# A two-layer spectral and MLP kernel: other PSUM banks for the zero multiplies between the layers

## The chip, the cores and the metric

The kernel runs on one core of one Trainium2 chip. The metric is the device time of one execution in microseconds, as the median of several runs. A profile is one further execution, recorded instruction by instruction. The engines are named as in the profile: PE is TensorE (its matrix multiplies), PEld are the weight loads of the same engine, DVE is VectorE, ACT is ScalarE, POOL is GpSimd, SP is SyncE, which issues most of the DMAs.

## The reference

The input is a state x of 2048 rows by 512 columns in bf16. Two kinds of layer follow each other, twice:

```
x = x + _A_ref(_layernorm(x), A_w_r, A_w_i)           # rfft2, times a complex weight, irfft2
x = x + _B_ref(_layernorm(x), B_w1, B_w2, B_w3, B_w4) # gelu MLP with row shifts, then an MLP of width 1792
x = x + _A_ref(_layernorm(x), A_w_r, A_w_i)
x = x + _B_ref(_layernorm(x), B_w1, B_w2, B_w3, B_w4)
```

`_A_ref` is a two-dimensional Fourier transform over the 2048 rows and 512 columns, an elementwise product, and the transform back. `_B_ref` is a layernorm, a 512 by 512 product with gelu, shifts of the rows by one or two in each quarter of the columns, a second 512 by 512 product, a residual, a layernorm, and an MLP of width 1792.

## The kernel before

The 2048 rows lie in SBUF as 128 partitions times 16 "rows" q, so that `x_state` is a tile of 128 x 16 x 512. The Fourier transform over the rows is split in two: a product over the 128 partitions (`over_p`, lines 361 and 363, or `over_p_plain`, line 373), and later one over the 16 values of q. The layernorm ahead of the transform is folded in: the statistics of row q give a factor, and `scale_T` multiplies the Fourier table T by it into a tile `Tq` (line 348, on DVE). The multiply with `Tq` as the moving operand then does norm and transform at once.

The function `layer` runs twice. Each call works through a long list of operations written out by hand, ORDER_A for the first call and ORDER_B for the second. The list sets the order of the instructions on every engine: an engine takes its own instructions in that order, and only semaphore waits hold it up. An entry is a letter for the function, a number for the piece of work, often V or A for DVE or ACT, and after a point the PSUM bank in which the result lies. PSUM is one tile `ps` of 8 banks of 512 fp32 columns. An operation that fills two banks takes the named one and the next.

The end of ORDER_A belongs already to the Fourier transform of the second call. Its entries there are:

- `Q14`: `scale_T` for the piece 14, which is row 0 of the state. One DVE instruction on line 348.
- `O4.0`, `O6.3`, `O14.6`, `O15.7`: the products over the partitions, called fronts here. O4 (line 373) fills banks 0 and 1 with the rows 10 and 11, O6 (lines 361 and 363) banks 3 and 4, O14 bank 6, O15 bank 7.
- `G4A` and `G4V`: taking O4 out of PSUM. G4A is an ACT copy (line 151) of columns 256 to 511 of both banks into a tile `right`. G4V is `fold_V`: four DVE instructions (line 385) that add `right` to, and subtract it from, columns 0 to 255 of both banks, and write the tile `V`. It is called the fold here.
- `G6A`, `G14A`, `G15A` and `G15V`: copies of O6, of O14 and of one half each of O15 into `V`, on ACT (line 151) and DVE (line 149).
- `X4` and `X8`: zero multiplies (line 243). The function `fill` issues 4 or 8 multiplies of a tile of zeros by itself into columns 0 to 255 of the named bank. Nothing reads what they write.

The first entry of ORDER_B is `d15.3`: `over_d`, line 476, the product over the columns for the last block. Its weights are slices of `V` over all rows, so that it needs all of the copies and folds above. The rest of the second call hangs on it.

In this list `X4.0` stands behind G4A and ahead of G4V. The four zero multiplies write columns 0 to 255 of bank 0 before the fold reads them, so that the fold takes zeros for the left half of row 10. The tile framework sees the fold as a reader of what the zero multiplies wrote, and makes it wait for them. `X4.6` stands behind G14A, which reads the same bank 6, and is made to wait for that copy. `X8.2` writes bank 2, which nobody has read for a while.

Of the kernel before, what the change touches and what calls it, by code (L numbers as in the profile page):

```python
# [765 lines left out]
o12V U6 g20 W8.4 j6 W10.7 w21.1 g21 Q2 A5 B5 A10 L8 A8 W9.6 B10 L2 Q3 L15 A9 w25.4 g25 w23.6 w24.1 j5 L3 g23 B8 O1.3  # L766
L0 W11.7 j8 w27.5 j7 S1 G1A G1V A11 w22.3 g27 Q6 j10 Q0 B11 B9 j9 Q7 g24 j11 S2 Q9 g22 w26.0 O3.4 G3A Q4 Q5 Q10 O2.6
G3V G2A g26 W12.3 Q8 A12 G2V B12 j12 W15.5 A15 B15 j15 O0.3 G0A G0V S15 W13.7 A13 B13 j13 W14.2 Q11 O5.5 G5A S12 Q12
S13 Q15 O15.7 A14 B14 j14 S14 Q13 O4.0 G4A G15V O6.3 G6A X4.0 Q14 O14.6 G14A X4.6 G4V G15A X8.2
"""  # L770
ORDER_B = """
d15.3 d1.6 t15A d4.0 t1V q1.2 x1A d8.4 t4V t8A q15.6 x15A p1 q4.2 d12.0 t12A x4V p15 p4 d10.6 t10A b1.3 q12.1 x12V m1A
# [45 lines left out]
```

## Time and profile before

| What | us |
|---|---|
| median of 5 runs (354.36 to 354.87) | 354.82 |
| time of the profiled execution | 354.83 |
| its span, first to last instruction | 352.9 |
| PE busy in the span | 341.0 |
| ACT busy | 200.6 |
| DVE busy | 185.1 |
| PE idle just ahead of the zero multiplies at 188.18 | 0.69 |

The span is what lies between the first and the last instruction; 1.9 us of the execution lie around it. Times inside the profile count from the start of the span. A busy time is the union of an engine's instructions. Multiplies overlap in the pipeline, so the time between the starts of two neighbours says what one costs in a stream, and the duration of one (273 ns for one of 256 columns) is longer than that. A start follows from a wait: what an instruction waited for stands behind an arrow in a list of idle times.

### The profile page before, as it was taken

What the parts mean: (1) busy time and instruction counts of PE and PEld (TensorE: products, weight loads), DVE (VectorE), ACT (ScalarE), POOL (GpSimd) and SP (SyncE); (2) the same over time, 40 slices, a digit from 0 to 9 for tenths busy, and PEclk for the clock granted to TensorE, in tenths of its full rate; (3) what the DMA queues carried; (4) which work ended last, traced back from release to release, by engine and by line L of the source; (5) the groups of instructions that cost most, each with busy time, mean ns of one, the idle gap of its engine ahead of it and who ended that gap; (6) DMA issues with size and microseconds to landing.
All of it is one profiled execution on the core that took longest, in us unless ns stands there. A gap on an engine that the chain in (4) does not pass through costs nothing.

```text
span 352.9 us, 5586 instructions
## 1 busy us (share of the span) xinstructions
PE 341.0 (97%) x2124; PEld 188.8 (53%) x2124; DVE 185.1 (52%) x442; ACT 200.6 (57%) x355; POOL 68.2 (19%) x171
## 2 busy tenths in 40 slices
PE   8789899999999999999999999899999999999996
PEld 6667786444444444444557888544444444444442
DVE  4869989769270445176586988845732004001003
ACT  4989989585736406213416979976583660442400
POOL 1430037462030101001120004646050010000000
PEclk9999999999999999999999999999999999999999
DMA  7996936611030030300000000762004005101003
GB/s 226 265 304 229 365 123 120 119 31 31 1 61 0 0 61 12 77 0 2 1 2 0 2 2 2 121 105 59 17 2 90 0 0 106 45 0 46 0 30 104
DMA packets 47210, 24.35 MB, mean 69 GB/s; under 512 B 36816, under 2 KB 43984, under 8 KB 47184
## 3 DMA queue, kind: packets, MB, share of 16 engines
q1 hardware_dynamic: 46464, 21.84, 24.9%
q0 software_dynamic: 576, 2.11, 1.5%
q8 instruction: 16, 0.26, 0.3%
q14 instruction: 10, 0.08, 0.1%
q10 hardware_dynamic: 144, 0.07, 0.1%
HBM read 11.41 MB, written 2.10 MB: 38 GB/s over the span
## 4 chain that ended last, share of the span: by engine, by line
PE 79%; ACT 6%; DMA 5%; DVE 3%; issue 3%; SPq 1%; POOL 1%; POOLq 0%; DVEq 0%; ACTq 0%
PE ps L655 27%; PE ps L642 27%; PE ps L591 8%; PE ps L607 8%; ACT hT L151 2%; PE ps L476 2%; PE ps L540 2%; DVE x_state L560 2%; DMA W<-W 2%; ACT xn L270 1%; DMA x_state<-in_A_x_dram 1%; PE ps L500 1%; DMA xT<-xn 1%; PE ps L524 1%; PE ps L552 1%
## 5 line engine op out<-in xcount | busy, mean ns | idle before, releaser
L649 ACT ACTIVATE gT<-ps 128x1024 bf16<-128x1024 f32 x56 | 56.6, 1023 | 84.1 <-PE ps L642 81.0
L642 PE MATMUL ps<-xT,w 128*128 128x512 bf16 x448 | 99.3, 379 | 0.0
L655 PE MATMUL ps<-w,gT 128*128 128x512 bf16 x448 | 99.0, 379 | 0.0
L660 DVE TENSOR_TENSOR x_state<-ps,x_state 128x512 bf16<-128x512 f32 x32 | 21.5, 689 | 111.7 <-PE ps L655 111.7
L642 PEld LDWEIGHTS <-w 128*128 128x128 bf16 x448 | 43.8, 98 | 52.9
L655 PEld LDWEIGHTS <-gT 128*128 128x128 bf16 x448 | 43.7, 98 | 52.1
L615 DVE SCALAR_TENSOR_TENSOR xn<-xn,ln_c,ps 128x512 bf16<-128x512 bf16 x32 | 23.2, 745 | 18.1 <-PE ps L607 15.7
L270 ACT ACTIVATE junk<-xn 128x512 bf16<-128x512 bf16 x32 | 19.9, 624 | 16.8 <-DVE xn L615 16.8
L607 PE MATMUL ps<-w,hT 128*128 128x512 bf16 x128 | 29.1, 379 | 0.0
L591 PE MATMUL ps<-xT,w 128*128 128x512 bf16 x128 | 28.4, 379 | 0.4 <-DMA xT<-xn 0.4
L276 POOL TENSOR_SCALAR ln_mv<-ln_s 128x4 f32<-128x4 f32 x16 | 5.5, 344 | 90.7 <-DVE x_state L560 52.0
L560 DVE SCALAR_TENSOR_TENSOR x_state<-ps,x_state 128x512 bf16<-128x512 f32 x32 | 20.4, 685 | 2.6 <-PE ps L552 1.9
L257 DVE BATCH_NORM_STATS2 ln_st<-x_state 128x6 f32<-128x512 bf16 x28 | 18.7, 686 | 4.6 <-DMA x_state<-in_A_x_dram 4.4
L515 DVE TENSOR_TENSOR PB<-X,W 128x1024 bf16<-128x1024 bf16 (+1 forms) x40 | 21.0, 584 | 0.1
L591 PEld LDWEIGHTS <-w 128*128 128x128 bf16 x128 | 12.4, 98 | 15.7 <-issue 0.7
L607 PEld LDWEIGHTS <-hT 128*128 128x128 bf16 x128 | 12.5, 98 | 15.1
L270 ACT ACTIVATE xn<-x_state 128x512 bf16<-128x512 bf16 x32 | 19.7, 620 | 0.5 <-DVE x_state L560 0.2
L598 ACT ACTIVATE hT<-ps 128x512 bf16<-128x512 f32 x32 | 17.0, 601 | 1.4 <-PE ps L591 1.3
L540 PE MATMUL ps<-G,hT 128*128 128x256 bf16 x128 | 15.1, 273 | 2.1 <-DVE hT L149 1.2
L476 PE MATMUL ps<-FA,V 128*128 128x256 bf16 x128 | 16.1, 273 | 0.8 <-DMA W<-in_A_w_i_dram 0.8
L552 PE MATMUL ps<-Y,Tinv 128*128 128x256 bf16 x128 | 15.8, 272 | 0.7 <-DVE Y L149 0.5
L524 PE MATMUL ps<-TR,PB 128*128 128x128 bf16 x256 | 16.0, 219 | 0.0
(78 smaller groups left out, 389.5 us busy)
## 6 DMA issues: line engine op xcount, KB each, us to landing
w<-in_B_w_dram SPq DMA_DIRECT2D x2, 1792.0 KB, 12.0
W<-W POOLq DMA_DIRECT2D x4, 514.0 KB, 5.4
x_state<-in_A_x_dram SPq DMA_DIRECT2D x8, 256.0 KB, 6.5
out_dram<-x_state SPq DMA_DIRECT2D x16, 128.0 KB, 1.9
TR<-tab_TR SPq DMA_DIRECT2D x2, 512.0 KB, 5.7
w<-in_B_w_dram SPq DMA_DIRECT2D x2, 512.0 KB, 4.5
W<-in_A_w_r_dram SPq DMA_DIRECT2D x7, 128.5 KB, 5.7
W<-in_A_w_i_dram SPq DMA_DIRECT2D x7, 128.5 KB, 5.2
```

The lines of the kernel that those rows point to most:

```text
L270: K.nc.scalar.activation(out, src, ACT.Square, bias=0.0, scale=D ** -0.5, accum_out=self.s[:, i, 1:2])
L476: nc.tensor.matmul(oi[:, 1 - h], rhs=K.FA[:, t, h], lhsT=V[:, 2 * t + h, 2 * b:2 * b + 2].rearrange("d b q c -> d (b q c)"), start=(t == 0 ...
L515: nc.vector.tensor_tensor(t[:, :, 0:n], x, w, op=ALU.mult)
L540: nc.tensor.matmul(o[:, i, e * 256:(e + 1) * 256], lhsT=M[:, F, e, 2 * m + i, :], rhs=K.G[:, F, e, :], start=(F == 0 and e == 0), stop=(F ...
L560: nc.vector.scalar_tensor_tensor(K.x[:, q, :], ps.pop(("P", q)), 1.0, K.x[:, q, :], op0=ALU.mult, op1=ALU.add, accum_out=ln[g].s[:, i, 0:1])
L591: nc.tensor.matmul(o[:, i], lhsT=K.w1[:, t, j * P:(j + 1) * P], rhs=xT[g][:, :, t, :], start=(t == 0), stop=(t == 3))
L607: nc.tensor.matmul(o, lhsT=K.hT[:, j, st:st + P], rhs=K.w2[:, j, :], start=(j == 0), stop=(j == 3))
L615: nc.vector.scalar_tensor_tensor(xn[:, q, :], xn[:, q, :], ln[q // 4].c[:, q % 4:q % 4 + 1], ps.pop(("u", n)), op0=ALU.mult, op1=ALU.add, ...
L642: nc.tensor.matmul(o[:, i], lhsT=K.w3[:, c, t * P:(t + 1) * P], rhs=xT3[g][:, :, c, :], start=(c == 0), stop=(c == 3))
L649: nc.scalar.activation(gT[g][:, 2 * j:2 * j + 2, :], ps.pop(("w", k)), ACT.Gelu_apprx_tanh, bias=0.0, scale=1.0)
L655: nc.tensor.matmul(o, lhsT=gT[g][:, t, i * P:(i + 1) * P], rhs=K.w4[:, t, :], start=(t == 0), stop=(t == 13))
L660: nc.vector.tensor_tensor(K.x[:, q, :], ps.pop(("W", n)), K.x[:, q, :], op=ALU.add)
```

## The change

Three entries of ORDER_A name another bank. `fill` writes columns 0 to 255 of that bank, as before, and no other function is touched. The numbers and the order of the instructions on every engine stay the same.

```
-S13 Q15 O15.7 A14 B14 j14 S14 Q13 O4.0 G4A G15V O6.3 G6A X4.0 Q14 O14.6 G14A X4.6 G4V G15A X8.2
+S13 Q15 O15.7 A14 B14 j14 S14 Q13 O4.0 G4A G15V O6.3 G6A X4.2 Q14 O14.6 G14A X4.2 G4V G15A X8.0
```

The waits that the framework sets follow the banks:

- The first of the four multiplies of the first X4 no longer waits for ACT (G4A).
- The fold G4V no longer waits for PE. It still waits for ACT (`right`).
- O14's first weight load now waits for DVE (its `Tq`) and its first multiply for ACT. Before, the multiply waited for DVE alone.
- The second X4 no longer waits for ACT (G14A).
- X8's first weight load now waits for DVE (the fold, the last reader of bank 0), and its first multiply for ACT (G4A).
- The weight loads of d15 no longer wait for DVE. The first still waits for ACT.

```
 L243 Ldweights zeros
+L243 Matmult ps<-zeros 128x256
+...
+L243 Ldweights zeros [waits DVE_49]
 L243 Matmult ps<-zeros 128x256 [waits Activation_49]
...
-L476 Ldweights V [waits DVE_49,Activation_49]
+L476 Ldweights V [waits Activation_49]
...
-L385 TensorTensor V<-ps,right 128x2x32x4 [waits PE_49,Activation_49]
+L385 TensorTensor V<-ps,right 128x2x32x4 [waits Activation_49]
```

## The prediction

> **What bounds the kernel now.** I read the page first for the bound, then the chain of waits around the place of the change, then the timeline there, and last PE's waits behind it, to see whether a gain would reach the end. The page says that PE decides:
>
> ```profile
> PE 341.0 (97%) x2124; PEld 188.8 (53%) x2124; DVE 185.1 (52%) x442; ACT 200.6 (57%) x355; POOL 68.2 (19%) x171
> ```
>
> PE is busy in 341.0 of 352.9 us, so what shortens PE's queue or its few gaps shortens the kernel, and 11.9 us are all its gaps together. The change touches one stretch of some 3 us. The chain that ended last, asked for between 183 and 190 us, shows who decides there:
>
> ```profile
> 186.55 0.02 issue
> 186.57 1.57 ACT V L151 x2
> 188.14 0.04 issue
> 188.18 1.47 PE ps L243 x12
> 189.65 0.44 PE ps L476 x4
> ```
>
> PE's fronts end, ACT makes the two copies G6A and G14A until 188.14, 0.04 us later twelve zero multiplies start (the second X4 and X8), and behind them d15 starts the second layer. So the zero multiplies stand on the path: the first of them waits for a copy because it writes that copy's bank. The timeline of the same stretch gives the durations (start, length, engine, line; in brackets the idle time before and who ended it):
>
> ```profile
> 186.42 0.60 PE L243 MATMUL ps<-zeros 128*128 128x256 bf16 x4
> 186.56 0.29 DVE L348 TENSOR_SCALAR Tq<-T,ln_r 128x256 bf16<-128x256 bf16 x1 [0.48 <-POOL ln_r L294]
> ...
> 186.90 0.27 PE L361 MATMUL ps<-Tq,x_state 128*128 128x256 bf16 x1
> ...
> 187.13 1.42 DVE L385 TENSOR_TENSOR V<-ps,right 128x256 bf16<-128x256 f32 x4 [0.28 <-PE ps L243]
> 187.23 0.27 PE L363 MATMUL ps<-Tq,x_state 128*128 128x256 bf16 x1
> ...
> 188.18 1.47 PE L243 MATMUL ps<-zeros 128*128 128x256 bf16 x12 [0.69 <-ACT V L151]
> ...
> 189.49 0.38 PE L476 MATMUL ps<-FA,V 128*128 128x256 bf16 x2
> ```
>
> Three things are to be seen. PE runs twelve zero multiplies from 188.18 to the start of d15 at 189.49, that is 1.31 / 12 = 0.109 us each. The fold (line 385) sat 0.28 us until the first four zero multiplies had ended at 187.02, and ran from 187.13 to 188.55. And d15's inputs, the fold and ACT's last copy (ACT's stretch of three copies ran from 186.57 for 1.84 us, to 188.41), were ready almost a microsecond before d15 began.
>
> **The change, part by part.** The sum is made against the profiled execution: a span of 352.9 and a time of 354.83, which lies 0.01 above the median of the runs.
>
> First X4, bank 2 for bank 0. Without its wait it starts 0.11 after the last multiply of O6 (186.26), at 186.37 for 186.42. That is worth nothing: O14 behind it waits for `Tq` from Q14, which ends at 186.56 + 0.29 = 186.85, and O14 began at 186.90 by that. Bank 2 was filled by W14 and read by DVE at 183.94 for 0.69 us, long before.
>
> O14's wait for DVE moves from its first multiply to its first weight load. In the trace of before two streams begin with a weight load that really waited, and they bound it:
>
> ```profile
> 21.97 0.22 PEld L476 LDWEIGHTS <-V 128*128 128x128 bf16 x3 [1.08 <-ACT V L151]
> 21.98 0.39 PE L476 MATMUL ps<-FA,V 128*128 128x256 bf16 x2 [0.80 <-DMA W<-in_A_w_i_dram]
> ```
>
> ```profile
> 209.33 0.66 PEld L540 LDWEIGHTS <-hT 128*128 128x128 bf16 x7 [0.99 <-ACT hT L151]
> 209.34 0.83 PE L540 MATMUL ps<-G,hT 128*128 128x256 bf16 x6 [0.82 <-ACT hT L151]
> ```
>
> In both the multiply starts 0.01 us after its weight load. The other end is a load inside a stream, 189.38 to 189.49 for d15's first, 0.11 us. I take 0.01, the rows of a load that waited; the other only keeps the pace of the stream. O14 keeps its start, and its copy G14A stays behind G6A on ACT: no gain, no loss (at the far end 0.1 us on ACT, covered since d15 begins 0.7 us after ACT's last copy).
>
> [...]
>
> The fold. Its wait for PE goes; `right` was ready at 185.78 + 0.59 = 186.37. What is late next is its own engine: Q14 from 186.56 to 186.85. In the stretch at 182.47 three such scalings took 0.65 us together, (0.65 - 0.29) / 2 = 0.18 from one to the next, so the fold starts between 186.56 + 0.18 = 186.74 and 186.85, where 187.13 was. With 1.42 us it ends at 188.16 to 188.27. It could lose only if DVE had other work first, and the order of its instructions is unchanged.
>
> Second X4. Without its wait the four multiplies follow O14's last (187.23) at 187.34 and are issued by 187.78, inside what was PE's gap of 0.69 us. They leave the path: 4 x 0.109 = 0.44 us less behind the wait.
>
> X8, bank 0 for bank 2. It now waits for the fold instead of standing behind a wait for G14A. Queued behind its first weight load on PE is d15, and behind d15 all of the second layer. Release takes 0.05 (0.04 in the chain above; 186.85 to 186.90 at O14). So X8 starts at 188.21 to 188.32, and with 8 x 0.109 = 0.87 and 0.01 for the load d15 starts at 189.09 to 189.20, against 189.49. ACT's last copy at 188.41 is not what ends last, even if a tenth late.
>
> d15's loads lose their waits for DVE. In the stream they already follow at 0.11 us (1.74 us for 16 at 189.38): nothing.
>
> Sum: 0.29 to 0.40 us earlier; I take 0.34, the middle. If the load did cost its 0.11, it would be 0.19 to 0.30. The most that this place can give is 0.40, since the eight multiplies stay behind the fold.
>
> Does it reach the end? PE waited for another engine three times after 189 us:
>
> ```profile
> PE ps L540 <- ACT hT L151: 0.8, 1, 0.8
> PE ps L552 <- DVE Y L149: 0.5, 1, 0.5
> PE ps L591 <- DMA xT<-xn: 0.4, 1, 0.4
> ```
>
> ACT, DVE and the transposing DMA there all work on what d15 began, so they move with it. The one load from outside, G2, is issued at the end of the first layer, and is used at 209 us. I let the whole gain through: 354.83 - 0.34 = 354.49, say 354.5. That is 0.1% below before, and about 0.2%, or 0.7 us, is what a measurement of this kernel can tell from no change. So the forecast is: faster by less than can be told.
>
> **The rivals.**
>
> *The wait changes its name and nothing is won.* X8 now waits for the fold, and if the fold is not released earlier, by its wait for `right` or an unseen one, it ends at 188.55 as now. Then d15 starts at 188.55 + 0.05 + 0.87 + 0.01 = 189.48, for 189.49: 354.8; with the 0.11 for a weight load 354.9. Against it speaks the bracket in the fold's row, which names PE alone, and that `right` was there 0.76 us before.
>
> *The gain is taken back behind d15.* The second layer's start is a chain through ACT, DVE and the transposes. If one of those keeps its old time, 354.8. For it speaks that PE waits 0.4 us for a transpose there; against it, that its input hangs on d15 too. It could also go the other way: the waits of 0.8, 0.5 and 0.4 us shrink because work falls better, together at most 1.7 us. Half of them with the 0.34 would be 353.6. Nothing in the profile speaks for that.
>
> *PE slows down between the layers: slower.* At the start the first 26 zero multiplies took 421 ns each and one came every 0.21 us, until 6.5 us; later ones take 273 ns at 0.109:
>
> ```profile
> L243 PE MATMUL ps<-zeros x26: 393/421/421, 1.0 to 6.3; 128*128 128x256 bf16 x26
> ...
> L243 PE MATMUL ps<-zeros x19: 272/273/407, 6.3 to 8.4; 128*128 128x256 bf16 x19
> ```
>
> If the gap between the layers brought that state back, 5.5 us of the start of the second layer would go at 0.21 for 0.109, a loss of 5.5 x (1 - 0.109 / 0.21) = 2.6 us: 357.1. It decides from an idle stretch longer than the ones that did no harm: 0.99 us ahead of the multiply at 9.68, and 0.69 here. After the change the last multiply of the second X4 starts at 187.67 and ends at 187.94, and X8 starts by 188.3, so PE idles for less than 0.4 us: the stretch gets shorter, and the slow state would have to come from another place.
>
> That the change does not do what it says can be left out: the waits of the built program differ as told above.
>
> **How the numbers follow.** The forecast, a gain of 0.2 to 0.4 us, has 0.64; nothing won or taken back, 0.18; a gain above 0.7 us, from the waits behind or from the spread of the runs, 0.10; a slower clock or an unseen wait that costs over 0.7 us, 0.08. The runs of before spread from 354.36 to 354.87 by themselves, so a gain of 0.34 put on them gives 354.0 to 354.5, and no gain 354.4 to 354.9. The range holds both, 354.0 to 354.95, and leaves out the fast and the slow case. With 0.7 us as the bound, the first two cases, less the 0.05 in which a gain of 0.3 meets a fast median, are the same: 0.77. Faster has 0.10 + 0.05 = 0.15 and slower 0.08.
>
> **What would show it.** In the changed kernel's profile: the fold starts by 186.85 after Q14, with no idle time put down to PE; the zero multiplies stand in two groups, four right behind O14 and eight from about 188.3 after an idle stretch ended by DVE; d15's first multiply is at 189.1 to 189.2; the three waits of PE behind it are unchanged, and the span is 352.5 to 352.6. A fold that still starts at 187.1, a first zero multiply of X8 0.1 us behind its load, zero multiplies of 421 ns, or a larger wait for the transposes would each make the forecast wrong at that step.

## The result, and the profile after

The changed kernel took 353.68 us (median of 35 runs), the kernel before 354.22 in 69 runs beside it. The ratio is 0.9984 with a 95% interval of 0.9978 to 0.9990, a gain of 0.57 us, between 0.35 and 0.78. That is within 0.2% of no change, as forecast, but the time itself lies below the forecast range of 354.0 to 354.95. The profiled execution took 353.59 us with a span of 351.7.

PE's gaps are still 11.9 us together (351.7 - 339.8), and it is busy 1.2 us less than before. That lies ahead of the change: the zero multiplies at the start of the program ended at 7.42 us, before at 8.69.

```profile
PE 339.8 (97%) x2124; PEld 188.0 (53%) x2124; DVE 184.8 (53%) x442; ACT 200.8 (57%) x355; POOL 68.4 (19%) x171
```

The chain that ended last, in the stretch of the change, no longer runs through ACT's copies. It comes from the statistics on DVE and POOL through Q14's scaling and the fold to the eight zero multiplies of X8, and then d15:

```profile
185.96 0.29 DVE Tq L348
186.24 1.34 DVE V L385 x4
187.58 0.05 issue
187.63 1.05 PE ps L243 x8
188.67 1.42 PE ps L476 x13
```

The timeline of the same stretch of the changed kernel:

```profile
185.96 0.29 DVE L348 TENSOR_SCALAR Tq<-T,ln_r 128x256 bf16<-128x256 bf16 x1 [0.48 <-POOL ln_r L294]
...
186.16 1.41 DVE L385 TENSOR_TENSOR V<-ps,right 128x256 bf16<-128x256 f32 x4
186.29 0.10 PEld L361 LDWEIGHTS <-x_state 128*128 128x128 bf16 x1 [0.21 <-DVE Tq L348]
186.30 0.28 PE L361 MATMUL ps<-Tq,x_state 128*128 128x256 bf16 x1
...
186.75 0.60 PE L243 MATMUL ps<-zeros 128*128 128x256 bf16 x4
187.62 0.77 PEld L243 LDWEIGHTS <-zeros 128*128 128x128 bf16 x8 [0.56 <-DVE V L385]
187.63 1.05 PE L243 MATMUL ps<-zeros 128*128 128x256 bf16 x8 [0.28 <-DVE V L385]
...
188.51 0.60 PE L476 MATMUL ps<-FA,V 128*128 128x256 bf16 x4
```

The fold has no idle time ahead of it. Both weight loads that now wait (186.29 and 187.62) are followed by their multiply after 0.01 us. X8 stands alone behind a wait for the fold, and d15 starts at 188.51.

The waits of PE behind the change are two of the old ones, and a smaller third:

```profile
PE ps L540 <- ACT hT L151: 0.8, 1, 0.8
PE ps L552 <- DVE Y L149: 0.5, 1, 0.5
PE ps L591 <- DMA xT<-xn: 0.2, 1, 0.2
```

Where did the 1.24 us between the two profiled spans go? PE's instructions are the same in number and order in both, so their starts can be subtracted one by one.

| Piece of the span | before | changed | difference |
|---|---|---|---|
| start to O14's first multiply | 186.90 | 186.30 | -0.60 |
| O14's first multiply to d15's first | 2.59 | 2.21 | -0.38 |
| d15 to the first product w1 (line 591) | 35.29 | 35.03 | -0.26 |
| w1 to the last multiply | 124.28 | 124.27 | -0.01 |

Only the second row is the change's own place. The first lies ahead of it, where the programs do not differ. The third holds the wait for the first transposes, 0.44 and 0.18 us. So the length from O14's first multiply to d15's first is the measure of all that follows, and the experiments below call it the stretch. It was 2.59 before and 2.21 in the changed kernel.

### The profile page after: what moved, and what is told of

Read it like the earlier page. It is cut to its first block, busy times and chain, and to the rows that moved or that the text cites. A ratio compares the mean times of both kernels' runs of the same rounds, so it can differ in the third digit from the quotient of the medians.

```text
span 351.7 us, 5584 instructions
## 1 busy us (share of the span) xinstructions
PE 339.8 (97%) x2124; PEld 188.0 (53%) x2124; DVE 184.8 (53%) x442; ACT 200.8 (57%) x355; POOL 68.4 (19%) x171
## 4 chain that ended last, share of the span: by engine, by line
PE 78%; DMA 6%; ACT 6%; DVE 4%; SPq 3%; issue 1%; POOL 0%; POOLq 0%; DVEq 0%; ACTq 0%
PE ps L655 28%; PE ps L642 27%; PE ps L591 8%; PE ps L607 8%; ACT hT L151 2%; PE ps L476 2%; DMA TL<-tab_TL 2%; DMA xT<-xn 2%; PE ps L540 2%; DVE x_state L560 2%; ACT xn L270 1%; DMA W<-W 1%; PE ps L500 1%; DMA W<-in_A_w_i_dram 1%; PE ps L524 1%
```

## The experiments

My theory: d15 starts at the later of two ends, the last of its inputs and PE's queue of zero multiplies, and what it gains passes to the end one to one. Rivals: something behind d15 adds to the gain (0.57 measured for 0.38 in the stretch); the clock needs the zero multiplies; the fold's wait alone is what counts.

### The second X4 alone

```
-... G6A X4.0 Q14 O14.6 G14A X4.6 G4V G15A X8.2
+... G6A X4.0 Q14 O14.6 G14A X4.2 G4V G15A X8.2
```

> The kernel before with one of the three new banks alone: the second X4 writes bank 2, the first stays on bank 0 and X8 on bank 2. As before, the fold takes zeros for the left half of row 10. Measured from O14's first multiply to d15's first: 2.59 us before, 2.21 in the changed kernel. Theory (the path is the later of the fold's end and PE's queue of zero multiplies): the twelve multiplies follow O14 without a wait, 0.44 + 12 x 0.109 = 1.75, and the fold, not released earlier, ends 1.65 after O14's first multiply, 1.70 with its release. d15 comes 1.75 to 1.76 us after O14, 0.84 earlier than before: ratio 0.9976. So one third of the change gives twice the gain of the whole. Rival (the stretch is amplified behind d15, 0.57 measured for 0.38 in the stretch): the same 1.75 there, but 1.26 us in the time, ratio 0.9964. Rival (nothing but the level of the runs differs): ratio near 0.9984 or 1.

Measured: 1.74 us from O14 to d15, ratio 0.9976 (0.9965 to 0.9986). The timeline of this kernel:

```profile
186.13 1.42 DVE L385 TENSOR_TENSOR V<-ps,right 128x256 bf16<-128x256 f32 x4 [0.28 <-PE ps L243]
186.22 0.27 PE L363 MATMUL ps<-Tq,x_state 128*128 128x256 bf16 x1
186.33 1.47 PE L243 MATMUL ps<-zeros 128*128 128x256 bf16 x12
...
187.64 0.82 PE L476 MATMUL ps<-FA,V 128*128 128x256 bf16 x6
```

The fold still waits 0.28 us for PE and does not matter. The twelve multiplies run straight behind O14, and d15 follows. The ratio is what 0.84 us makes, 353.98 - 0.84 being 353.14 for a measured median of 353.04. The interval leaves out 1.26 us (0.9964) by a little.

### All zero multiplies on bank 2

```
-... G6A X4.2 Q14 O14.6 G14A X4.2 G4V G15A X8.0
+... G6A X4.2 Q14 O14.6 G14A X4.2 G4V G15A X8.2
```

> The changed kernel with one part undone: X8 writes bank 2 as before, so that none of the zero multiplies waits for a reader. Theory: the fold starts as in the changed kernel, 0.14 us ahead of O14's first multiply, and ends 1.27 after it; the twelve multiplies follow O14 directly and end the queue at 0.45 + 12 x 0.109 = 1.76 us. d15 then starts 1.76 us after O14's first multiply, where it was 2.21 in the changed kernel and 2.59 before: 0.45 earlier than the first and 0.83 than the second, ratio to before 0.9977. Rival (amplified behind d15 by 1.5): 1.25 us, 0.9965. Rival (the fold, not PE's queue, decides, and X8's bank is of no account): 2.21 as in the changed kernel, ratio 0.9984 to 0.9989.

Measured: 1.76 us, ratio 0.9979 (0.9967 to 0.9992). So X8's new bank 0, and with it the wait for the fold, costs 0.45 us in the stretch. The rival that X8's bank is of no account falls.

### No zero multiplies between the layers

```
-... G6A X4.2 Q14 O14.6 G14A X4.2 G4V G15A X8.0
+... G6A Q14 O14.6 G14A G4V G15A
```

> The changed kernel without any of the 16 zero multiplies between the layers; the output needs none of them. Theory: d15 then waits for the last of its inputs. The fold ends 1.27 us after O14's first multiply, ACT's last copy 1.52 after it, so d15 starts at 1.57, 1.02 earlier than before and 0.64 earlier than in the changed kernel: ratio to before 0.9971, and PE idles 0.96 us. Rival (clock): the idle stretch brings the slow multiplies of the first 6 us back, 421 ns each, up to 2.6 us lost, so 1.6 us slower than before: ratio 1.004 to 1.005. Rival (amplified by 1.5): 1.5 us, 0.9957.

Measured: 1.57 us, ratio 0.9973 (0.9961 to 0.9986). The timeline of this kernel at d15:

```profile
187.98 0.66 PEld L476 LDWEIGHTS <-V 128*128 128x128 bf16 x7 [1.24 <-ACT V L151]
187.99 0.83 PE L476 MATMUL ps<-FA,V 128*128 128x256 bf16 x6 [0.96 <-ACT V L151]
```

d15 waits for ACT's last copy, as worked out, and 0.96 us of idle PE brings no slow multiplies: d15's first sixteen took 1.92 us together, 1.91 in the changed kernel, where PE idled 0.28 us ahead of X8. The clock rival falls at this place. By medians this kernel, 353.14 us for 353.98 before, also beats the changed one, and its output needs none of the zeros. The kernel with all zeros on bank 2 (353.34) does nearly as well. These medians of 12 runs each are too close to rank the two.

### Sixteen behind the fold

```
-... G14A X4.2 G4V G15A X8.0
+... G14A X4.2 G4V G15A X16.0
```

> The changed kernel with X8 doubled to sixteen zero multiplies behind the fold. Theory: eight more at 0.109 us are 0.87 us on the path, so d15 starts 3.08 us after O14's first multiply, 0.49 later than before and 0.87 later than in the changed kernel: ratio to before 1.0014. Rival (the zero multiplies are hidden by something else that d15 waits for): 2.21 as in the changed kernel, 0.9984 to 0.9989. Rival (amplified by 1.5): 0.73 us slower than before, 1.0021.

Measured: 3.08 us, as worked out, but a ratio of 1.0047 (1.0029 to 1.0066, six runs), 1.7 us for the 0.49. The expectation for the time was wrong. The timeline of PE in this kernel shows a second loss 50 us behind d15:

```profile
240.66 0.60 PE L591 MATMUL ps<-xT,w 128*128 128x512 bf16 x2 [0.77 <-DMA xT<-xn]
```

The trace's DMA records point to a cause. The two transposes issued at 234.9 and 236.2 us moved their packets from 236.1 to 240.1 us (4.1 us), where the changed kernel took 3.3 us for the same pair. The longest packet took 1.76 us instead of 0.98. Into this time falls one packet of 16 KB of the queue that the page lists as "q8 instruction", at 237.4 us. In the changed kernel that packet came at 239.3 us, 1.5 us after the pair was done. The queue reads 0.26 MB in 16 packets, some 62 bytes for each of PE's 4250 instructions, so I take it for PE's code; that is my inference from the size, and the trace does not name an engine for it. The place of the packet goes with the length of PE's program: in the kernel without zero multiplies, 32 instructions shorter, it came 54.4 us behind d15, in the changed kernel 50.8, here 47.4. Why sixteen instructions more and 32 fewer move it by about as much is not worked out. A smaller packet, 8 KB of another instruction queue (q14), lies inside the same pair in the changed kernel too, at 236.2 us, without a wait of PE. The kernel here has sixteen PE instructions more (eight multiplies and their weight loads). My expectation for the next kernel says 32 more; that number is wrong, it is sixteen.

### The same sixteen without longer code

```
-... G6A X4.2 Q14 O14.6 G14A X4.2 G4V G15A X8.0
+... G6A Q14 O14.6 G14A G4V G15A X16.0
```

> Tells why sixteen zero multiplies behind the fold cost 1.7 us for the 0.49 worked out. Here both X4 are left out and X8 is sixteen, all on bank 0 behind the fold: the same wait and the same sixteen on the path, but PE's program has as many instructions as before and as changed. Theory (the path takes its 0.49, and the rest came from PE's code: with 32 instructions more, the read of the next 16 KB of PE's instructions met the transposing DMAs, 237.4 us against 236.1 to 240.1, and they landed 0.77 us later): d15 again 3.08 us after O14's first multiply, no meeting, the read about 50 us behind d15 as in the changed kernel: ratio to before 1.0014. Rival (what d15 loses is amplified behind it): 1.0047 again.

Measured: 3.08 us and a ratio of 1.0022 (1.0011 to 1.0033). The packet comes 50.9 us behind d15, the pair's packets end 49.3 behind it, and PE no longer waits there. Timeline of this kernel at the same place:

```profile
238.36 1.03 PE L607 MATMUL ps<-w,hT 128*128 128x512 bf16 x4
239.39 3.63 PE L591 MATMUL ps<-xT,w 128*128 128x512 bf16 x16
```

1.0014 lies in the interval, 1.0047 does not. In the profile the wait went with the code's length, and from d15 to the last multiply it took 159.40 us, where the first kernel with sixteen took 160.08. So what d15 loses is not amplified. The times alone show less, as the repeat of the sixteen below tells.

### Eight more where PE idles anyway

```
-... b6.5 m14V m6A D3.6 D2.0 ...
+... b6.5 m14V m6A X8.6 D3.6 D2.0 ...
```

> The changed kernel with eight more zero multiplies at another place: into bank 6 ahead of the first product of the transform back in the second layer, where PE idles 0.82 us until ACT's copy is done. They cost the path 0.1 us at most, but make PE's program as long as that of the sixteen ahead of the transposes. Theory (code read meets the transposes): d15 2.21 us after O14's first multiply as in the changed kernel, the read of PE's instructions starts while the transposes of the second pair run, PE waits about 0.8 us for them as with the sixteen: ratio to before 1.0006 to 1.0013. Rival (the length of the program is of no account): as the changed kernel, 0.9984 to 0.9992.

Measured: 2.21 us, ratio 1.0022 (1.0008 to 1.0037). The code packet comes 47.4 us behind d15, as with the sixteen, the pair's packets run from 46.0 to 50.0, and PE waits again:

```profile
238.45 1.90 PE L591 MATMUL ps<-xT,w 128*128 128x512 bf16 x8 [0.69 <-DMA xT<-xn]
```

Eight zero multiplies that stand in a gap, and leave d15 and the transform back where they were, bring nearly the same wait. The rival that the program's length is of no account falls: its 0.9984 to 0.9992 is outside the interval. The account of the profile, -0.38 + 0.69 = 0.31 us, gives 1.0009, at the low edge of the interval.

### The changed kernel and the sixteen once more

The changed kernel again:

> The changed kernel itself on this chip beside the others. Theory (what d15 gains passes to the end one to one): 0.38 us, ratio 0.9989. Rival (something behind d15 adds to it, as the 0.57 measured first would say): 0.9984 or lower.

Measured: 2.21 us, ratio 0.9994 (0.9980 to 1.0008). The theory's 0.9989 is inside; this run alone can't tell it from 0.9984, nor from no gain.

The sixteen with both X4 again:

> The sixteen behind the fold with both X4 kept, once more. Theory (code read meets the transposes): 1.004 to 1.005 again, and the trace shows PE's instruction read inside the transposes of the second pair and a wait of PE of about 0.8 us there. Rival (an accident of six runs): 1.0014.

Measured: 3.08 us, PE waits 0.77 us for the second pair again, with the code packet 47.3 us behind d15. The ratio is 1.0026 (1.0013 to 1.0040), lower than expected. The stretch and the wait give 0.49 + 0.77 = 1.26 us, 1.0036, which lies in the intervals of both runs of this kernel; but the accident of six runs (1.0014) lies in this interval too, and beside the same kernel before the sixteen without longer code had 1.0022, so that the times do not tell the two apart. The wait itself is not an accident: it stands in all three profiles with the longer code, and in none of the ten others. From d15 to the last multiply those three took 159.99 to 160.08 us, the ten others 159.28 to 159.57. The packet was not moved without the length of the program, so that the meeting of the two is the likely cause, and the wait with the longer program is what is shown.

### Single profiles: the kernel before, the first X4 alone, X8 alone

> The kernel before itself, one more profile, for the only place behind d15 where the two first profiles differ: PE's wait for the first transposes was 0.44 us before and 0.18 changed. Theory (one to one, the 0.26 is chance): about 0.2 here as in the profiles of all other kernels. Rival (the change itself shortens this wait, and that is why the first measurement gave 0.57 for 0.38): 0.4 to 0.5 again.

Measured in the kernel before: 2.59 us, and no wait for the first transposes in its list of waits of PE behind the change:

```profile
PE ps L540 <- ACT hT L151: 0.8, 1, 0.8
PE ps L552 <- DVE Y L149: 0.5, 1, 0.5
```

So the 0.44 us in the first profile of before is not a property of that kernel, and neither is the third row of the table above: from d15 to the last multiply this second profile took 159.32 us, the changed kernel 159.30.

```
-... G6A X4.0 Q14 O14.6 G14A X4.6 G4V G15A X8.2
+... G6A X4.2 Q14 O14.6 G14A X4.6 G4V G15A X8.2
```

> The kernel before with the first X4 alone moved to bank 2; the fold then reads the sums and no zeros. Theory: the fold starts 0.14 us ahead of O14's first multiply and ends 1.27 after it, 0.38 earlier, but the second X4 still waits for G14A, and twelve multiplies stand behind it: d15 at 2.59 us, as before. The earlier fold alone is worth nothing. Rival (the fold's wait is what the path hung on): 2.21.

```
-... G6A X4.0 Q14 O14.6 G14A X4.6 G4V G15A X8.2
+... G6A X4.0 Q14 O14.6 G14A X4.6 G4V G15A X8.0
```

> The kernel before with X8 alone moved to bank 0; as before, the fold takes zeros for the left half of row 10. Theory: the second X4 waits for G14A and takes its four places until 1.72 us after O14's first multiply; the fold ends at 1.65, 1.70 with its release, so that X8's new wait is over by then: d15 at 2.59 to 2.61, as before. Rival (a wait on the weight load costs 0.11): 2.7.

Measured, in one profile each: 2.60 us with the first X4 alone and 2.59 with X8 alone. In the first the fold ends 0.38 us earlier, but the twelve multiplies still stand behind G14A. In the second the fold ends before it is X8's turn. The timeline of the kernel with the first X4 alone:

```profile
186.46 1.41 DVE L385 TENSOR_TENSOR V<-ps,right 128x256 bf16<-128x256 f32 x4
...
187.89 1.47 PE L243 MATMUL ps<-zeros 128*128 128x256 bf16 x12 [0.69 <-ACT V L151]
...
189.20 0.82 PE L476 MATMUL ps<-FA,V 128*128 128x256 bf16 x6
```

And of the kernel with X8 alone:

```profile
186.82 1.42 DVE L385 TENSOR_TENSOR V<-ps,right 128x256 bf16<-128x256 f32 x4 [0.28 <-PE ps L243]
...
187.88 1.47 PE L243 MATMUL ps<-zeros 128*128 128x256 bf16 x12 [0.68 <-ACT V L151]
...
189.18 1.04 PE L476 MATMUL ps<-FA,V 128*128 128x256 bf16 x8
```

Neither gains, though the second X4 alone gains 0.84. The three parts are not a sum: the second X4 opens the way, and X8's new bank gives half of it back. What the first X4 adds to the other two was not run without it. By the theory it decides there how much X8 gives back, since it lets the fold end 0.38 us earlier.

## Why the prediction was right and where it was wrong

**The stretch.** Each step of the working came out. Counted from O14's first multiply (186.90 before), the fold was to start 0.05 to 0.16 us ahead of it and started 0.14 ahead; X8's load was to cost 0.01 and cost 0.01; d15 was to come at 2.19 to 2.30 and came at 2.21. The gain is 0.38 us for 0.34 taken, with 0.29 to 0.40 as bounds. A weight load of 128 columns took 95 to 99 ns in this stretch, before and in the changed kernel. The multiply did not start that much later: it came 0.01 us behind the start of the load that had waited, at O14 and at X8, and at X8 the next one followed after 0.12 us, 0.01 more than in a stream. The sentence "The most that this place can give is 0.40" holds only with the eight multiplies behind the fold; without any zero multiplies the stretch was 1.01 us shorter than before.

**The rivals.** A fold that is not released, a clock that falls and a gain that is taken back did not happen. The first and second are settled by the profile after and by the kernel without zeros. In the changed kernel the granted clock was 1.00 from 186 to 194 us. That a longer idle stretch could bring the slow multiplies back was my assumption: no run shows an idle stretch to be their cause, and 0.96 us between the layers brought none. For the third, d15 to the last multiply took 159.30 us in the changed kernel and 159.57 and 159.32 in the two profiles of before: nothing is taken back there. The wait for the first transposes, forecast as unchanged, was 0.18 us for 0.44, which the second profile of before shows to be no gain of the change.

**One to one.** Three kernels with 0.83 to 1.01 us in the stretch gained 0.64 to 0.94 in their medians. The changed kernel's 0.57 has 0.38 just inside its interval (0.35 to 0.78), and the repeat was smaller, 0.35 by medians and 0.21 by the ratio. Nothing behind d15 need be added. In the kernels that were slower the time lies above the account of the profile in three of four runs, by 0.3 to 0.6 us and within the intervals; whether anything stands behind that stays open.

**The step that failed** is the level that the gain was put on: the 354.83 in "354.83 - 0.34 = 354.49", and with it the range, "The runs of before spread from 354.36 to 354.87 by themselves, so a gain of 0.34 put on them gives 354.0 to 354.5". Five runs were taken for the level and the spread of the kernel before. In 69 runs, those five among them, its median is 354.22, 0.61 below the base of the sum, and they reach from 353.14 to 355.19. The sum missed the measured 353.68 by 0.81 us: 0.61 is this level, and 0.20 is what the gain by medians, 0.54, had above 0.34. The span, forecast as 352.5 to 352.6, was 351.7 in the same way: 0.60 us of what the two profiles differ by lies ahead of O14. The range should have been put on a ratio, or made wider by the spread that a kernel shows between runs.

Whether the five runs came out high by their small number or by something else about that series is not shown. In the two later series of the experiments the same kernel had medians of 353.98 and 353.83.

The profiles show where executions differ. The first product w1 of the first layer started between 56.42 and 58.14 us in thirteen profiles, although no kernel differs ahead of it. From there to O14's first multiply it was 129.27 us in all thirteen. The spread comes with the loads and the first transposes, ahead of everything that the change touches. PE's first product started between 8.57 and 9.84 us, behind statistics of DVE that waited for the load of x, and in two of the profiles PE waited 0.41 and 0.43 us more for the first transposes, just ahead of w1.

## What to carry to other kernels

A filler on the critical engine is free only while its own wait is: before it is given another buffer, ask who read that buffer last and where that reader ends, since here one of three new banks took back 0.45 us of the 0.84 that another gave. Work out a small gain from the last two ends at the place where they meet, and test the parts alone, because they don't add up. And give a forecast of a tenth of a percent as a ratio: five runs of a kernel do not fix its level to that.

## What the runs showed of the hardware

- A program longer by sixteen PE instructions had a 16 KB packet of the instruction queue in the middle of a pair of transposes, in three profiles of three, and PE waited 0.69 to 0.77 us for that pair. The pair's packets took 4.0 to 4.1 us, in the ten other profiles 3.3. In one of the three the added instructions stood in a gap of PE and put nothing on the path themselves. That the two transfers slow each other is my reading and not shown; the trace does not show which DMA engine carried what.
- In the first profile of the sixteen the granted clock fell near the start: PE idled 2.53 us ahead of its first product, ran 0.7 us at a granted clock of 1.00 and then 3.4 us at 0.51, where its multiplies took 0.42 us for 0.27. Idle stretches of 1.98 and 2.17 us at the same place in two other profiles, the first X4 alone and all zeros on bank 2, were followed by multiplies of 271 and 272 ns and a granted clock of 1.00. One case does not show that the idle time was the cause. The first block is the line of the timeline. In the second, each stretch and its length are followed by the busy times of PE, PEld, DVE, ACT and POOL with their instructions, then the granted clock (1.00, then 0.51), the DMA share and GB/s.

```profile
9.84 0.27 PE L361 MATMUL ps<-Tq,x_state 128*128 128x256 bf16 x1 [2.53 <-DVE Tq L348]
```

```profile
9.00:10.50 1.50, 0.66 (x7) 0.59 (x7) 1.46 (x6) 1.00 (x3) 0.00 (x0) 1.00 1.13 350
10.50:14.00 3.50, 3.50 (x19) 2.52 (x17) 2.79 (x12) 3.50 (x13) 0.85 (x4) 0.51 0.73 200
```

It cost nothing there: the first w1 started at 57.66 us, and at 57.64 in the profile of before, whose granted clock was 1.00 from 9 to 30 us.
